# The opening's last chain in single-bank PSUM tiles, one A unit ahead of step 0 instead of two, step 0 in halves

## The chip, the cores and the metric

The kernel runs on one core of one Trainium2 chip. The metric is the device time of one execution in microseconds (us); it is given as the median of several runs. All times inside an execution are from one profiled execution, counted from its first instruction. The engines are named as in the profile: PE (TensorE's matmuls), PEld (its weight loads), DVE (VectorE), ACT (ScalarE), POOL (GpSimd) and SP (SyncE, which here only issues DMAs).

## The reference

`x` holds 8 images of 3008 rows with 256 columns. Each image is transformed along its rows, mixed by a complex 256x256 matrix, shrunk towards zero and transformed back; all rows then go through a two-layer network with an ELU between.

```python
X = np.fft.rfft(x, axis=1)                       # x: (8, 3008, 256)
Yr = Xr @ w_r - Xi @ w_i + b_r
Yi = Xr @ w_i + Xi @ w_r + b_i
Yr = np.sign(Yr) * np.maximum(np.abs(Yr) - 0.01, 0.0)   # Yi likewise
y = np.fft.irfft(Yr + 1j * Yi, n=3008, axis=1)
h = y.reshape(24064, 256) @ w_in                 # w_in: (256, 2048)
g = np.where(h > 0.0, h, np.exp(np.minimum(h, 0.0)) - 1.0)
out = g @ w_out                                  # w_out: (2048, 256)
```

## The kernel before

**Units.** The Fourier transforms are done as matmuls, 3008 being 47 x 64. Per image there are five kinds of units, each a few matmuls into a PSUM tile that ACT or DVE then copies (evicts) to SBUF:

- A (6 per image, `unit_A`, line 146): the first transform of `x`. Two units fill one tile `A` of 8 columns, which SP stores to the DRAM tensor `DA` (line 159). `A` comes from a pool with two buffers of tag `A`, so the tile after next can be written only when the store has read this one.
- X (8, `unit_X`): the second transform, from `Z`, which is `DA` read back in another layout (`load_Z`, two loads).
- M (12, `unit_M`): the complex mixing and the shrinking, giving `Y`.
- B (6, `unit_B`, line 246): the first inverse transform, into `Bz`, stored by SP to the DRAM tensor `DB`.
- Y (8, `unit_Y`, line 347): the second inverse transform, from `Bs`, which is `DB` read back (`load_Bs`, four loads `w` = 0 to 3), into `yT`.

**Opening.** Image 0 goes through all of its units before the first step. The order of the opening is written out by hand, and every engine and SP's DMA queue run their instructions in that order. B units 0, 1 and 2 of image 0 are needed soonest; `turn_B` and `turn_back` take them to `Bs` by small matmuls instead of through DRAM. Then come Y units 0 and 1, `fB(2)` (B unit 2 for the other rows, whose store completes `DB`), and the three remaining loads of `Bs`. `spare_A(0)` and `spare_A(1)` are A units 0 and 1 of image 1, done in the gaps; `spare_A(1)` also issues the store of that tile to `DA`, ahead of the loads of `Bs` in SP's queue. PSUM is held in the opening by `pre2` (two tiles of two banks), `pre1` (three of one) and `pre0` (one). `unit_ps("tps", True)` and `unit_ps("yps", True)` are tiles of two banks, whose halves ACT and DVE copy.

**Steps.** The network is then worked off in 376 steps, 47 per image. Step `i` (`front`, line 790) computes one pair of 128 hidden columns for a block of 512 rows: four matmuls into `hps`. ACT takes its exponential into `Et`; then either DVE clamps it (line 829) and forms `gT` (line 817), or, in a step without other work ("bare"), ACT, POOL and DVE do it in halves (lines 799, 827 and 815). Two steps later `back` (line 848) multiplies `gT` into the output. PSUM now has `psF` (one tile of two banks, for the units), `psH` (two of two, for `hps`) and `psO` (two of one).

**Who works beside the steps.** `plan(b)` writes out, for the 47 steps beside image `b`, which unit goes into which step: kind `a` (A units of the next image, only for `b` = 0) and the loads come in `f1`, after the step's `hps` matmuls; all others in `f0`, before them. For `b` = 0 the order is: A units 2 to 5 of image 1 in steps 0 to 3, Y units 2 to 7 of image 0, X, M and B units of image 1, A units 0 to 2 of image 2, Y units 0 and 1 of image 1 (called `n`), A units 3 to 5 of image 2; three steps are left bare. The loads of `Bs` for image 1 follow its B unit 5, the loads of `Z` follow the last A unit.

Of the kernel before, what the change touches and what calls it, by code (L numbers as in the profile page):

```python
# [10 lines left out]
BF16 = mybir.dt.bfloat16  # L11
# [8 lines left out]
N1 = 47  # L20
# [9 lines left out]
def kernel(  # L30
# [53 lines left out]
    xtp = ctx.enter_context(tc.tile_pool(name="xtp", bufs=1))  # L84

    ctx.enter_context(tc.manual_schedule())
    first = ExitStack()
    pre2 = first.enter_context(tc.tile_pool(name="pre2", bufs=2, space=bass.MemoryType.PSUM))
    pre1 = first.enter_context(tc.tile_pool(name="pre1", bufs=3, space=bass.MemoryType.PSUM))
    pre0 = first.enter_context(tc.tile_pool(name="pre0", bufs=1, space=bass.MemoryType.PSUM))  # L90
# [182 lines left out]
        nc.sync.dma_start(Bs[r0:], dv[r0:, 8 * w : 8 * w + 8, :])  # L273
        Bs_of[b, w] = Bs

    def spare_A(u):

        got = []
        if u == 0:
            A_of[1, 0] = wk2.tile([P, 8, D], BF16, name="A", tag="A")  # L280
            DA_of[1] = dram.tile([NJ, P, D], BF16, name="DA", tag="DA")
        for j in range(2):
            ps = pre1.tile([P, 512], F32, name="aps1", tag="mps1")
            c = 4 * u + 2 * j
            nc.tensor.matmul(ps[:], lhsT=M1[:], rhs=xts[0][:, c : c + 2, :], start=True, stop=True)
            got.append((A_of[1, 0][:, c : c + 2, :].rearrange("p n d -> p (n d)"), ps))

        def store(first_on_dve):
            for j, (A, ps) in enumerate(got):
                evac(A, ps[:], first_on_dve or bool(j))  # L290
            if u:
                nc.sync.dma_start(DA_of[1][0:8].rearrange("j p d -> p j d"), A_of[1, 0][:])

        return store

    NT = 3
    turned = []

    def turn_B(v):

        if not turned:
            turned.append(wk3.tile([P, 2, 8, 16 * NT], BF16, name="yb", tag="yb"))
        Y, T = Y_of[0, v], turned[0]
        ps = unit_ps("tps", True)
        to = ps[:, :, 0:P].rearrange("p s (t m q g) -> p s t q g m", t=2, m=8, q=2)
        for pp in range(2):
            for dt in range(2):
                for c in range(2):
                    for s in range(2):
                        nc.tensor.matmul(  # L310
                            to[:, s, dt, pp],
                            lhsT=Y[
                                s * N2 : s * N2 + N2, pp, c * D + dt * P : c * D + dt * P + P
                            ],
                            rhs=M3[s * N2 : s * N2 + N2, 2 * v + pp, c, :].rearrange(
                                "p (g m) -> p g m", g=4
                            )[:, :, 0:8],
                            start=(c == 0), stop=(c == 1),
                        )
        Tv = T[:, :, :, 16 * v : 16 * v + 16].rearrange("p t m (q s g) -> p s (t m) q g", q=2, s=2)  # L320
        fr = ps[:, :, 0:P].rearrange("p s (n q g) -> p s n q g", q=2, g=4)
        for s, copy in enumerate((nc.scalar.copy, nc.vector.tensor_copy)):
            copy(Tv[:, s], fr[:, s])

    def turn_back(dt):

        ps = unit_ps("tps", True)
        for j in range(8):
            nc.tensor.matmul(
                ps[0 : 16 * NT, j // 4, j % 4 * P : j % 4 * P + P],  # L330
                lhsT=turned[0][:, dt, j, :], rhs=idm[:], start=True, stop=True,
            )
        for h, copy in enumerate((nc.scalar.copy, nc.vector.tensor_copy)):
            copy(
                Bs_of[0, 0][0 : 16 * NT, 4 * h : 4 * h + 4, dt * P : dt * P + P],
                ps[0 : 16 * NT, h, :].rearrange("p (m d) -> p m d", d=P),
            )

    def unit_Y(b, u, alone=False, on_dve=False):
        w, dt = u // 2, u % 2  # L340
        if u == 0:
            yT_of[b] = late2.tile([P, 2, S], BF16, name="yT", tag="yT")
        yT, Bs = yT_of[b], Bs_of[b, w]
        ps = unit_ps("yps", alone)
        psv = ps[:].rearrange("p a (k j) -> p (a k) j", j=P)
        for j in range(8):
            nc.tensor.matmul(  # L347
                psv[:, j, 0 : 2 * N1], lhsT=Bs[:, j, dt * P : dt * P + P], rhs=M4[:],
                start=True, stop=True,
            )  # L350
        yv = yT[:, dt, w * WT : w * WT + WT].rearrange("p (r j) -> p r j", j=8)
        pv = psv[:, :, 0 : 2 * N1].rearrange("p j r -> p r j")
        if alone:
            for h in range(2):
                evac(yv[:, h * N1 : h * N1 + N1], pv[:, h * N1 : h * N1 + N1], bool(h))
        else:
            evac(yv, pv, on_dve)

    busy = constp.tile([P, 512], BF16, name="busy")
    nc.vector.memset(busy[:], 1.0)  # L360
# [307 lines left out]
    def fB(v, on_dve=False):  # L668
        unit_B(0, v, alone=True, on_dve=on_dve)
# [54 lines left out]
    first_M(2, 1, True)  # L724
    turn_B(1)
    let_go()
    fB(1, True)
    load_w_in(3)
    turn_B(2)
    spare_A(0)(False)  # L730
    M4v = M4[:].rearrange("p (a h) -> p a h", h=2)
    for h, w in enumerate((w40, w41)):
        nc.gpsimd.tensor_scalar(
# [1 line left out]
        )  # L735
    gate(Bs_of[0, 0][64:96, 0, 0:1])
    load_w_out(1)
    turn_back(0)
    turn_back(1)
    store = spare_A(1)  # L740
    unit_Y(0, 0, alone=True)
    idle_pe(1)
    unit_Y(0, 1, alone=True)
    fB(2)
    store(True)
    scale_w_in(1, True, 1)
    for w in range(1, 4):
        load_Bs(0, w)
    first.close()

    psF = ctx.enter_context(
        tc.tile_pool(name="psF", bufs=1, space=bass.MemoryType.PSUM, reuse_waits="tile")
# [122 lines left out]
    def plan(b):  # L875

        f0 = [[] for _ in range(PER)]
        f1 = [[] for _ in range(PER)]
        n1, n2 = b + 1, b + 2
        mid = [("X", u) for u in range(8)] + [  # L880
            ("M", 0, 0), ("M", 0, 1), ("M", 1, 0), ("M", 1, 1), ("B", 0), ("M", 2, 0),
            ("M", 2, 1), ("B", 1), ("M", 3, 0), ("M", 3, 1), ("B", 2), ("M", 4, 0),
            ("M", 4, 1), ("B", 3), ("M", 5, 0), ("M", 5, 1), ("B", 4),
            ("A", 0), ("B", 5), ("A", 1), ("A", 2), ("A", 3), ("A", 4),
        ]
        if n1 < B:
            lead, seq = 0, [("y", u) for u in range(2, 6)] + mid
            if b:
                seq.insert(20, ("y", 6))
                seq.insert(24, ("y", 7))  # L890
                xs = (3, 8, 13)
                seq += [("A", 5), ("n", 0), ("n", 1)]
            else:
                seq = (
                    [("a", u) for u in range(2, 6)] + [("y", u) for u in range(2, 8)]
                    + [u for u in mid if u[0] != "A"]
                    + [("A", 0), ("A", 1), ("A", 2), ("n", 0), ("n", 1)]
                    + [("A", u) for u in range(3, 6)]
                )
                xs = (9, 12, 15)  # L900
        else:
            lead, seq = 0, [("y", u) for u in range(2, 8)]
        for t, u in enumerate(seq, lead):
            if u[0] == "y":
                f0[t].append(put("Y", b, u[1]))
            elif u[0] == "n":
                f0[t].append(put("Y", n1, u[1]))
            elif u[0] == "a":
                f1[t].append(put("A", n1, u[1]))
            elif u[0] == "A":  # L910
                if n2 < B:
                    f0[t].append(put("A", n2, u[1]))
            else:
                f0[t].append(put(u[0], n1, *u[1:]))
            if u == (("A", 1) if b and n2 < B else ("B", 5)):
                f1[t] += [(load_Bs, (n1, w)) for w in range(4)]
            if u == ("A", 5) and n2 < B:
                f1[t] += [(load_Z, (n2, s0, s1)) for s0, s1 in ((0, 8), (8, NS))]
        if b == 0:
            for t in range(4):  # L920
                f1[t + 1].append((scale_w_in, (2 + t // 2, True, t % 2)))
            f1[4] += [(load_Z, (1, s0, s1)) for s0, s1 in ((0, 8), (8, NS))]
            f1[xs[0]].append((lambda: gate(Z_of[1][:, 16, 0:1]), ()))
        if n2 < B:
            for ci in range(3):
                f1[xs[ci]].append((load_x, (n2, ci)))
        return f0, f1
# [3 lines left out]
    for i in range(n + LAG):  # L931
        if i < n:
            r = i % PER
            if r == 0:
                f0, f1 = plan(i // PER)
                used = [bool(u0 or u1) for u0, u1 in zip(f0, f1)]
            free = not used[r]
            bare = bare + 1 if free else 0
            calm = free and (i >= n - 2 or (r + 2 < PER and not used[r + 1] and not used[r + 2]))
            for f, a in f0[r]:  # L940
                f(*a)
            on_act = any(f is unit_M for f, a in f0[r])
            h = front(i, calm and bare % 3 == 1, on_act, free and i > 0)
        finish_elu()
        if i < n:
            for f, a in f1[r]:
# [1 line left out]
            split = i > LAG and (i - LAG) % NPAIR == NPAIR - 1  # L948
            if split:
                back(i - LAG, True)  # L950
            elu(i, *h, free and i > 0, on_act)
        else:
            split = False
        if i >= LAG and not split:
# [31 lines left out]
```

## Time and profile before

| | us |
|---|---|
| median of 3 runs | 910.41 (909.49 to 911.92) |
| profiled execution, its own time | 909.7 |
| its span, first to last instruction | 907.9 |
| first matmul of step 0 (line 790) | 54.07 |
| eviction of A unit 4 of image 1 on ACT | 60.25 |
| first Y unit beside the steps (line 347) | 63.57 |
| Y unit 0 of image 1 (line 347) | 148.12 |

A line of the timeline has the start, the duration, the engine, the source line, the operation, what it writes and reads, the shapes and the count of instructions merged; in brackets the time for which the engine stood idle before it, and what released it. "SPq" is SP issuing DMAs. A line of the windows has, for each engine, busy time and count, then the granted PE clock (1.00 is full), the DMA engines' share and GB/s. A piece of the chain of waits has start, duration and what the time went to. When a DMA has landed is in the trace's landing records, which no view prints for each DMA; where such a time is used, the text says so.

### The profile page before, as it was taken

The numbers are of one execution on the slowest core, as the hardware profiler recorded it, in microseconds if no ns is written. First come the engines' busy times: TensorE is split into PE (matmuls) and PEld (weight loads), VectorE is DVE, ScalarE is ACT, GpSimd is POOL, SyncE is SP. The second block draws the span as 40 slices with busy tenths as digits, with TensorE's granted clock in tenths as the row PEclk, the third lists the DMA queues.
The fourth block names the chain that finished last, engine by engine and source line by source line (L and its number), as shares of the span: only waits on it lengthen the run. The fifth ranks groups of instructions, "written<-read, shape, count | busy, mean of one in ns | idle before, by whom it ended". The sixth has DMA issues, their size and how long they took to land.

```text
span 907.9 us, 17273 instructions
## 1 busy us (share of the span) xinstructions
PE 885.0 (97%) x6665; PEld 653.1 (72%) x6768; DVE 721.0 (79%) x901; ACT 698.9 (77%) x855; POOL 313.0 (34%) x436
## 2 busy tenths in 40 slices
PE   9879999999999999999999999999999999999997
PEld 3457667876678676876678766787667866777775
DVE  8779778887788778887788877888778877778776
ACT  6678778787878788788787888878787877777664
POOL 7700440233331431405404153133332134443664
PEclk9999999999999999999999999999999999999999
DMA  8997025721383215722176031752228111221011
GB/s 270 310 258 233 24 70 174 222 70 48 93 232 117 70 48 155 199 88 93 53 204 186 25 106 58 205 167 80 61 73 229 32 40 47 84 80 48 24 47 47
DMA packets 90623, 106.06 MB, mean 117 GB/s; under 512 B 5270, under 2 KB 81308, under 8 KB 87180
## 3 DMA queue, kind: packets, MB, share of 16 engines
q1 hardware_dynamic: 84284, 77.42, 30.5%
q0 software_dynamic: 5968, 27.26, 9.1%
q8 instruction: 53, 0.87, 0.4%
q10 hardware_dynamic: 288, 0.26, 0.1%
q14 instruction: 30, 0.25, 0.1%
HBM read 55.12 MB, written 49.81 MB: 116 GB/s over the span
## 4 chain that ended last, share of the span: by engine, by line
PE 84%; DVE 5%; ACT 4%; DMA 3%; issue 2%; POOL 0%; SPq 0%; DVEq 0%; ACTq 0%; POOLq 0%
PE ps_o L848 34%; PE hps L790 33%; PE mps L194 9%; PE yps L347 2%; PE bps L246 2%; PE aps L146 2%; PE xps L177 2%; DVE gT L817 1%; ACT Bz L259 1%; ACT Et L804 1%; DMA Bs<-DB 1%; DVE Et L829 1%; DMA Z<-DA 1%; ACT Et L801 1%; DMA DB<-Bz 1%
## 5 line engine op out<-in xcount | busy, mean ns | idle before, releaser
L848 PE MATMUL ps_o<-w_out_r,gT 128*128 128x256 f32 x3008 | 476.9, 301 | 0.2 <-DVE gT L815 0.2
L848 PEld LDWEIGHTS ps_o<-w_out_r,gT 128*128 128x128 f32 x3008 | 403.6, 189 | 49.9 <-DVE osb L859 1.3
L790 PE MATMUL hps<-yT,w_in_s 128*128 128x512 bf16 (+7 forms) x1651 | 382.3, 351 | 6.6 <-ACT Bz L259 1.1
L815 DVE SCALAR_TENSOR_TENSOR gT<-Et,hps 128x512 fp32r<-128x512 f32 (+1 forms) x268 | 220.3, 850 | 74.1 <-POOL Et L827 37.6
L817 DVE SCALAR_TENSOR_TENSOR gT<-hps,Et 128x1024 fp32r<-128x1024 f32 x200 | 244.6, 1223 | 16.2 <-DVE Et L829 0.5
L790 PEld LDWEIGHTS <-w_in_s 128*128 128x128 bf16 x1728 | 141.6, 98 | 129.7 <-issue 22.7
L804 ACT ACTIVATE Et<-hps 128x1024 f32<-128x1024 f32 x200 | 206.1, 1030 | 11.1 <-PE hps L790 4.4
L827 POOL TENSOR_SCALAR Et<-Et 128x512 f32<-128x512 f32 x183 | 109.2, 615 | 219.4 <-ACT Et L799 219.4
L829 DVE TENSOR_SCALAR Et<-Et 128x1024 f32<-128x1024 f32 x200 | 138.6, 693 | 48.0 <-ACT Et L804 39.9
L212 POOL TENSOR_SCALAR clip<-yb 128x512 f32<-128x512 f32 x84 | 51.8, 616 | 318.1 <-DVE yb L204 286.0
L799 ACT ACTIVATE Et<-hps 128x512 f32<-128x512 f32 x184 | 99.9, 595 | 62.8 <-PE hps L790 62.1
L801 ACT ACTIVATE Et<-hps 128x1024 f32<-128x1024 f32 x84 | 86.2, 1027 | 71.8 <-PE hps L790 70.2
L213 POOL TENSOR_TENSOR Y<-yb,clip 128x512 bf16<-128x512 f32 x84 | 107.3, 1277 | 7.0
L802 ACT ACTIVATE Et<-Et 128x1024 f32<-128x1024 f32 x84 | 88.9, 1058 | 2.7
L204 DVE TENSOR_TENSOR yb<-mps,bias_bc 128x512 f32<-128x512 f32 x89 | 61.3, 689 | 35.5 <-PE mps L194 23.2
L129 ACT CAST XT<-xps 128x768 bf16<-128x768 f32 x61 | 48.8, 799 | 15.4 <-PE xps L177 15.4
L129 ACT CAST yT<-yps 128x752 bf16<-128x752 f32 (+1 forms) x64 | 49.8, 779 | 13.4 <-PE yps L347 13.2
L129 ACT CAST A<-aps 128x1024 bf16<-128x1024 f32 (+1 forms) x47 | 47.2, 1004 | 13.2 <-PE aps L146 11.6
L194 PE MATMUL mps<-wcat_r,XT 128*128 128x512 bf16 x180 | 55.6, 384 | 0.8 <-ACT Bz L259 0.3
L194 PE MATMUL mps<-wcat_s,XT 128*128 128x512 bf16 x182 | 54.9, 379 | 0.7
L194 PEld LDWEIGHTS <-XT 128*128 128x128 bf16 x384 | 30.8, 98 | 29.6 <-DVE XT L127 0.6
L259 ACT CAST Bz<-bps 128x1024 bf16<-128x1024 f32 x46 | 46.1, 1001 | 2.8 <-PE bps L246 2.8
(121 smaller groups left out, 414.3 us busy)
## 6 DMA issues: line engine op xcount, KB each, us to landing
xt<-in_x_dram POOLq DMA_DIRECT2D x21, 1024.0 KB, 7.5
out_dram<-osb SPq DMA_DIRECT2D x158, 128.0 KB
Bs<-DB SPq DMA_DIRECT2D x31, 384.0 KB
DA<-A SPq DMA_DIRECT2D x21, 512.0 KB
DB<-Bz SPq DMA_DIRECT2D x21, 512.0 KB
Z<-DA SPq DMA_DIRECT2D x7, 1152.0 KB
Z<-DA SPq DMA_DIRECT2D x11, 384.0 KB
xt<-in_x_dram POOLq DMA_DIRECT2D x6, 512.0 KB, 5.8
```

Source lines behind the costliest of these rows:

```text
L129: nc.scalar.copy(dst, src)
L194: nc.tensor.matmul(ps, lhsT=XT[:, dt, c, o : o + P], rhs=wm[:, dt, :], start=(not biased and m == 0 and dt == 0), stop=(m == 1 and dt == 1),)
L213: nc.gpsimd.tensor_tensor(Y_of[b, q][:, i, :], yb, clip[:], ALU.subtract)
L790: nc.tensor.matmul(hps[:, s, c0:c1], lhsT=w_in_s[:, dt, ft * P : ft * P + P], rhs=yT_of[b][:, dt, t0 : t0 + c1 - c0], start=(dt == 0), sto ...
L799: nc.scalar.activation(E_[:, s], hps[:, s], AF.Exp)
L801: nc.scalar.activation(E_, hps[:], AF.Relu, scale=-1.0)
L804: nc.scalar.activation(E_, hps[:], AF.Exp)
L815: nc.vector.scalar_tensor_tensor(o, e, -1.0, h, ALU.add, ALU.max)
L817: nc.vector.scalar_tensor_tensor(o, h, 0.0, e, ALU.max, ALU.add)
L827: eng.tensor_scalar(E_[:, s], E_[:, s], 1.0, 0.0, ALU.min, ALU.max)
L829: nc.vector.tensor_scalar(E_, E_, 1.0, -1.0, ALU.min, ALU.add)
L848: nc.tensor.matmul(po[q][:, i_ % 2, :], lhsT=gT[:, s, i_ * P : i_ * P + P], rhs=w_out_r[:, ft, :], start=(ft == 0 and i_ % 2 == 0), stop=( ...
```

## The change

- `spare_A` loses its argument: only A unit 0 of image 1 is done ahead, into two single-bank tiles (`lateA`), copied by ACT and DVE. It issues no store. A unit 1 goes to the front of `plan(0)`: units 1 to 5 of kind `a` take steps 0 to 4, and the store of the first tile `A` is issued by unit 1, in step 0. All that follows in `plan(0)` up to B unit 5 comes one step later; of the A units of image 2, two instead of three stand ahead of `n`, and four behind it. The loads of `x` and `Z` move one step too. Two steps are left bare.
- From `turn_B(2)` on, the opening uses PSUM pools of single banks: `lateA` (2), `chain` (4) and `lateB` (2). ACT copies one bank and DVE another. These banks are later `psF`, `psH` and `psO`, in this order.
- `turn_B(0)` and `turn_B(1)` are copied by ACT alone, `fB(1)` too.
- `fB(2)` becomes `last_B(2)`, which comes after the first Y units on PE, in two single banks copied by DVE.
- `first_Y` replaces `unit_Y(0, 0)` and `unit_Y(0, 1)`; its halves are four of the eight columns each. `idle_pe(1)` between them is gone.
- Step 0 is done in halves, as a bare step is.

```diff
-    def spare_A(u):
+    def two_banks(pool, n):
+        return [pool.tile([P, 512], F32, name=n, tag=n) for _ in range(2)]
+
+    def spare_A():
...
-            if u:
-                nc.sync.dma_start(DA_of[1][0:8].rearrange("j p d -> p j d"), A_of[1, 0][:])
+    def last_B(v):
+
+        Bz, Y = Bz_of[0, v // 2], Y_of.pop((0, v))
+        ps = two_banks(lateB, "lateB")
...
+        def store():
+            for s in range(2):
+                evac(Bv[:, s], ps[s][:].rearrange("p (q d) -> p q d", d=D), True)
+            nc.sync.dma_start(
+                DB_of[0][4 * v : 4 * v + 4].rearrange("k p d -> p k d"), Bz[:, o : o + 4, :]
+            )
...
-        for s, copy in enumerate((nc.scalar.copy, nc.vector.tensor_copy)):
-            copy(Tv[:, s], fr[:, s])
+        for s in range(2):
+            evac(Tv[:, s], ps[s].rearrange("p (n q g) -> p n q g", q=2, g=4), split and bool(s))
...
+    def first_Y(dt):
...
+        for h in range(2):
+            ps = one_bank()
+            pv = ps[:].rearrange("p (k j) -> p k j", j=P)[:, :, 0 : 2 * N1]
+            for j in range(4):
+                nc.tensor.matmul(
+                    pv[:, j], lhsT=Bs_of[0, 0][:, 4 * h + j, dt * P : dt * P + P], rhs=M4[:],
+                    start=True, stop=True,
+                )
+            evac(yv[:, :, 4 * h : 4 * h + 4], pv.rearrange("p j r -> p r j"), bool(h))
...
-    fB(1, True)
+    fB(1)
     load_w_in(3)
-    turn_B(2)
-    spare_A(0)(False)
...
     load_w_out(1)
+    first.close()
+    lateA, chain, lateB = (
+        second.enter_context(
+            tc.tile_pool(name=n_, bufs=k_, space=bass.MemoryType.PSUM, reuse_waits="tile")
+        )
+        for n_, k_ in (("lateA", 2), ("chain", 4), ("lateB", 2))
+    )
+    turn_B(2, True)
     turn_back(0)
     turn_back(1)
-    store = spare_A(1)
-    unit_Y(0, 0, alone=True)
-    idle_pe(1)
-    unit_Y(0, 1, alone=True)
-    fB(2)
-    store(True)
+    keep_A = spare_A()
+    first_Y(0)
+    first_Y(1)
+    keep_B = last_B(2)
+    keep_A()
+    keep_B()
     scale_w_in(1, True, 1)
     for w in range(1, 4):
         load_Bs(0, w)
-    first.close()
+    second.close()
...
-                    [("a", u) for u in range(2, 6)] + [("y", u) for u in range(2, 8)]
+                    [("a", u) for u in range(1, 6)] + [("y", u) for u in range(2, 8)]
                     + [u for u in mid if u[0] != "A"]
-                    + [("A", 0), ("A", 1), ("A", 2), ("n", 0), ("n", 1)]
-                    + [("A", u) for u in range(3, 6)]
+                    + [("A", 0), ("A", 1), ("n", 0), ("n", 1)]
+                    + [("A", u) for u in range(2, 6)]
                 )
-                xs = (9, 12, 15)
+                xs = (10, 13, 16)
...
-            f1[4] += [(load_Z, (1, s0, s1)) for s0, s1 in ((0, 8), (8, NS))]
+            f1[5] += [(load_Z, (1, s0, s1)) for s0, s1 in ((0, 8), (8, NS))]
...
-            h = front(i, calm and bare % 3 == 1, on_act, free and i > 0)
+            h = front(i, calm and bare % 3 == 1, on_act, free or i == 0)
...
-            elu(i, *h, free and i > 0, on_act)
+            elu(i, *h, free or i == 0, on_act)
```

## The prediction

> **What bounds the kernel now.** I read the page first, then the chain of waits, then the timeline of the opening, of SP's queue and of the PE.
>
> ```profile
> PE 885.0 (97%) x6665; PEld 653.1 (72%) x6768; DVE 721.0 (79%) x901; ACT 698.9 (77%) x855; POOL 313.0 (34%) x436
> ```
>
> PE is busy for 885 of 907.9 us: time is won only where PE waits, and a wait put into PE's queue is paid in full. PE waits in the opening (48 to 64 us), which the change rewrites:
>
> ```profile
> 49.28 1.06 ACT L334 CAST Bs<-tps 48x512 bf16<-48x512 f32 x2 [0.30 <-PE tps L329]
> 49.89 1.28 DVE L334 CAST Bs<-tps 48x512 bf16<-48x512 f32 x2 [0.57 <-ACT Bs L334]
> 51.75 1.10 DVE L127 CAST yT<-yps 128x376 bf16<-128x376 f32 x2 [0.58 <-ACT yT L129]
> 53.01 1.01 ACT L259 CAST Bz<-bps 128x1024 bf16<-128x1024 f32 x1 [0.73 <-PE bps L246]
> 54.07 1.02 PE L790 MATMUL hps<-yT,w_in_s 128*128 128x512 bf16 x4 [1.10 <-ACT Bz L259]
> 60.25 1.00 ACT L129 CAST A<-aps 128x1024 bf16<-128x1024 f32 x1
> 62.51 1.00 ACT L129 CAST A<-aps 128x1024 bf16<-128x1024 f32 x1
> 63.57 0.49 PE L347 MATMUL yps<-M,Bs 96*128 96x94 bf16 x8 [0.59 <-ACT A L129]
> ```
>
> DVE's half of an eviction begins when ACT's half ends (0.57, 0.58), and step 0's matmuls (54.07) wait for the eviction of `fB(2)`, whose banks they take. 63.57 is the first Y unit of the steps, y2; I call its time the landmark. Now SP's queue:
>
> ```profile
> 54.04 0.36 SPq L262 DMA_DIRECT2D DB<-Bz  x1
> 54.46 0.50 SPq L292 DMA_DIRECT2D DA<-A  x1
> 58.15 1.26 SPq L273 DMA_DIRECT2D Bs<-DB  x3
> 59.51 4.41 SPq L159 DMA_DIRECT2D DA<-A  x2
> ```
>
> SP issues nothing from 54.96 to 58.15: the loads of `Bs` wait there for the store of `DB`. The first store of `DA` (columns 0 to 7 of image 1) stands before that wait. The trace's landing records give 58.08 for `DB`, 59.47 for this `DA`, 62.01, 64.82 and 65.88 for the three `Bs`, and 67.18 for the next `DA`.
>
> **The change, part by part.**
>
> *The chain to step 0.* Until `turn_back` little moves: ACT takes both halves of `turn_B(0)` and `(1)` and all of `fB(1)`, which I cost at nothing, as PE runs units of its own meanwhile; `turn_back` then starts near 48.2 (before: 48.61). If ACT's extra halves (3 of 0.27) show, it is 0.4 later. From there DVE is the slower lane. PE: `turn_back` 1.07 to 49.27, two matmuls of A 0.47 to 49.74. DVE: its first `Bs` half ends by about 50.15, the first `yT` half can start at 49.74+0.53 (a matmul group's start to its eviction, 50.72 to 51.25) = 50.27, two halves of 0.55: 51.37. Step 0's matmuls start at 51.4 instead of 54.07; not later than 51.9 if the strided `yT` writes cost more. The 8 matmuls of `last_B` (0.61) run under these evictions, and its own evictions now leave other banks than step 0's.
>
> *Five A units instead of four.* Before, step 0 to the landmark takes 63.57-54.07 = 9.50 with four. One more such step is 2.26 (58.27 to 60.53), and step 0 in halves takes back about 0.1 of it (ACT 1.09, POOL 1.19, DVE 1.28 overlap, gT is 0.5 earlier, but ACT's evictions follow one another anyway): 11.7. The landmark would be at 51.4+11.7 = 63.1: 0.5 gained.
>
> *The A unit after the first stage.* It falls among bare steps: a step with A takes 2.30 (155.51 to 157.81), a bare one 1.83 (157.81 to 159.64): 0.47 more.
>
> *n0.* Unit B5 moves one step towards n0, the first Y of image 1, since only two A units stand between.
>
> ```profile
> 139.31 1.03 ACT Bz L259
> 140.36 3.24 DMA DB<-Bz
> 143.73 4.35 DMA Bs<-DB
> 148.12 0.51 PE yps L347 x8
> ```
>
> From B5's eviction to n0 it takes 7.8 whatever PE does. PE's wait there grows from 0.3 to about 2.6, by the A step that is taken away. It adds nothing to the sum: n0 keeps its distance from B5, and B5 from the landmark.
>
> *The store of DA, the term that decides.* In the changed kernel this store is no longer issued by `spare_A`, but by unit 1 in step 0, after the three `load_Bs` in SP's queue. It is passed by all three and stands behind their wait for `DB`. Who waits for it: unit 4's eviction writes the buffer of tag `A` (two buffers) from which this store reads; before, it ran at 60.25, 0.8 after the store had landed. In the built order of the changed kernel ACT's copy of unit 4 waits on that store's semaphore; behind it on ACT stand step 4's Exp and unit 5's eviction, and PE waits for both.
>
> The sum: `yT` done on DVE 51.37, then 0.64 and twice 0.64 for lateA and lateB: `DB` issued at 53.3, landed 4.04 later as before: 57.35. `Bs` x3 and then `DA` issued 1.43 later (58.08 to 59.51): 58.8. Behind three `Bs` loads a `DA` took 7.67 (59.51 to 67.18); behind four, 7.8 (145.73 to 153.53). I take off 0.66, half of the 1.3 in which the old first `DA` still ran beside those loads: landed at 65.8. The bounds: alone a `DA` took 4.33 (159.34 to 163.67), landing 63.1; with `DB` no earlier than now and 7.8, 67.3.
>
> Without this, unit 4's eviction would start at 51.4+8.4 (62.51-54.07) = 59.8. So ACT is held for 6.0. After the landing: eviction, Exp, eviction of unit 5 at intervals of 0.92, then y2: 2.9 later, at 68.7. Against 63.57 this is 5.1, with the 0.47 it is 5.6.
>
> What else moves with it is covered: step 0's two clamps go to POOL, which is idle from 50 to 66; the loads of `Z` follow the last `DA` (issued at 68.7, then 5.1 as at 63.5, then 4.1 and 8.6 for the two parts, as landed at 72.99 and 77.53 after 68.88), so 78 and 82.4, while X0 comes 12.9 after the landmark as before, at 81.6, and the unit that needs the second part 4.5 later. If that cover were gone, each us would count in full.
>
> *The clock.* PE stands still from about 60.9 (end of step 4's hps) to 66.9, six us.
>
> ```profile
> 1.45 4.02 PE L366 MATMUL ips<-busy 128*128 128x512 bf16 x9 [1.45 <-DVE busy L360]
> 8.17 0.82 PE L366 MATMUL ips<-busy 128*128 128x512 bf16 x3
> 904.00:905.00 1.00, 0.00 (x0) 0.00 (x0) 0.00 (x0) 0.00 (x0) 0.00 (x0) 0.96 0.40 99
> 905.00:906.00 1.00, 0.00 (x0) 0.00 (x0) 0.00 (x0) 0.00 (x0) 0.00 (x0) 0.50 1.03 325
> ```
>
> Nine matmuls at the start take 4.02, later the same matmul takes a little over 0.2; the fast rate comes at about 7.2, after 5.8 of work. At the end PE's last matmul ends at 902.6, and the granted clock (the column behind the engines) is 0.96 at 904 to 905 and 0.50 after. The gap of 1.55 at 24 us left it at 1.00. So I expect half speed after six us of rest. With 5.8 at half speed, unit 5, the back step, y2, hps and a part of the next back step take double: 2.5 lost. If it lasts 3.4, 1.3 is lost; nothing at the least, 2.95 at the most.
>
> The Trainium skill (TensorE: Matmul & The Clock Gate, Part 1) puts both at about 3.4 us, idle to slow down and busy to come back. By its figure for coming back the loss would be 1.3 rather than 2.5.
>
> *Sum.* 0.5 earlier at step 0 is inside the landmark; 5.1+0.47+2.5 = 8.1. The profiled execution took 909.7 (span 907.9): 917.8. It lies 0.7 below the median of 910.41, so 918.5 for a median.
>
> **The rivals.** All in medians.
>
> A. As summed: 918.5. Chance 0.62.
>
> B. The same wait, but the clock holds: 910.4+5.6 = 916.0. For it: no gap inside the steps of before shows a slowdown; against it: none there is over two us, and the end of the span shows one. 0.18.
>
> C. The store isn't held by the loads before it and takes what it takes alone, 4.33: y2 at 63.1+2.9 = 66.0, 2.5+0.47 more: 913.4. Against it stand both rows of a `DA` behind `Bs` loads. 0.05. [...]
>
> D. Not slower: `DA` lands before 59.8, so unit 4 never waits. Then the landmark is at 63.1, and -0.5+0.47 is nothing: 910.4. The point that decides is this landing. It would need `DB` landed by about 51 or the store ahead of the loads; against it stands SP's queue, silent for 3.2 us in the fence above. 0.12, of which 0.03 for a gain over 0.3% because the chain to step 0 or the B units come out earlier than I see.
>
> E. `DB` lands no earlier than now, and the slow clock lasts longest: 67.3 and 2.95, some 920.5 and over. 0.03.
>
> **The numbers.** 0.3% of 910.4, 2.7 us, is about what a measurement can tell from no change: the same is 907.7 to 913.1. A, B, E and most of C are slower: 0.87; D without its fast part and the rest of C the same: 0.10; faster 0.03. The range goes from C, 913.2, to E, 920.5, and leaves out D and what is above: less than 2 in 10.
>
> **What would show it.** In the changed kernel: step 0's hps near 51.4; SP's second line after `DB` is `Bs` x3, with `DA` near 58.8; a wait of ACT's copy into `A` for the DMA of `DA`, about 6, and PE idle from 61 to 67; then matmuls of hps at 0.43 each and a granted clock under 1 for some us; y2 at 68.7 or later; PE's wait at n0 2 to 3 us; one bare step less in image 0. A copy of unit 4 before 60.5 would refute A, B, C and E at once; a wait with a clock of 1.00 throughout makes it B.

## The result and the profile after

The changed kernel takes 920.05 us (median of 6 runs, 918.23 to 921.62), the kernel before 910.5 (909.49 to 911.95) in the runs beside it: the ratio is 1.0102, interval 1.0085 to 1.0118. The profiled execution took 920.67 (span 918.9), 11.0 more than that of before.

First the page's busy time, for the changed kernel:

```profile
PE 893.4 (97%) x6767; PEld 655.0 (71%) x6767; DVE 719.8 (78%) x898; ACT 699.0 (76%) x857; POOL 313.0 (34%) x436
```

PE's sum is 8.4 us larger, but records of 102 more of its instructions are in it, so it doesn't measure the loss; DVE, ACT and POOL do what they did. The loss is found in the timeline.

The timeline of the changed kernel's opening, lines that answer to those shown of before:

```profile
48.12 0.41 PE L343 MATMUL one<-M,Y 64*128 64x32 bf16 x16 [1.21 <-ACT A L259]
...
49.67 1.28 DVE L127 CAST Bs<-one 48x512 bf16<-48x512 f32 x2 [0.79 <-PE one L362]
...
51.13 1.01 DVE L127 CAST yT<-one 128x376 bf16<-128x376 f32 x2 [0.18 <-PE one L380]
...
51.90 1.10 PE L839 MATMUL hps<-yT,w_in_s 128*128 128x512 bf16 x4
...
66.92 1.01 ACT L129 CAST A<-aps 128x1024 bf16<-128x1024 f32 x1 [6.35 <-DMA DA<-A]
...
67.98 1.22 PE L146 MATMUL aps<-xt,M 128*128 128x512 f32 x2 [6.19 <-ACT A L129]
...
69.00 1.91 PE L897 MATMUL ps_o<-w_out_r,gT 128*128 128x256 f32 x8
...
70.71 0.74 PE L394 MATMUL yps<-M,Bs 96*128 96x94 bf16 x8
```

The change does what it says: DVE no longer waits for ACT's half, and step 0 starts 2.2 earlier (51.90; 54.07 before). But by y2, the landmark, the 2.2 won have become 7.1 lost (70.71; 63.57). Between them stands one wait: ACT's copy of A unit 4 into `A`, held for 6.35 by a DMA, and PE behind it for 6.19. Its cause is in SP's queue:

```profile
53.95 0.36 SPq L317 DMA_DIRECT2D DB<-Bz  x1
58.64 1.26 SPq L273 DMA_DIRECT2D Bs<-DB  x3
59.95 10.69 SPq L159 DMA_DIRECT2D DA<-A  x3
```

The first `DA` store is issued at 59.95, behind the loads of `Bs`, which stood for 4.3 in the queue until `DB` had landed (58.56 in the landing records). The loads landed at 62.58, 64.22 and 65.46, the store at 66.82, 0.10 before ACT went on.

The windows of the changed kernel (busy time and count of PE, PEld, DVE, ACT and POOL, then the granted clock, the DMA engines' share and GB/s):

```profile
62.00:64.00 2.00, 0.00 (x0) 0.00 (x0) 1.00 (x2) 0.00 (x0) 0.00 (x0) 1.00 1.01 240
64.00:66.00 2.00, 0.00 (x0) 0.00 (x0) 0.00 (x0) 0.00 (x0) 0.00 (x0) 0.59 1.06 295
...
68.00:70.00 2.00, 2.00 (x7) 1.81 (x8) 1.01 (x2) 1.62 (x2) 0.00 (x0) 0.50 0.00 0
70.00:72.00 2.00, 2.00 (x18) 1.55 (x16) 0.91 (x1) 0.77 (x2) 0.00 (x0) 0.70 0.36 116
72.00:74.00 2.00, 2.00 (x21) 1.67 (x20) 0.59 (x1) 1.66 (x3) 0.00 (x0) 1.00 0.46 146
```

PE rests from 61.8. By the trace's clock records, whose mean the windows print, the clock is at half rate from 64.36 to 71.19: it halves some 2.5 after PE's last matmul and is back 3.2 after PE resumed (67.98). In between unit 5's two matmuls take 1.22 instead of 0.73. The second place is Y unit 0 of image 1 (n0), in the timeline and the windows:

```profile
155.81 0.51 PE L394 MATMUL yps<-M,Bs 96*128 96x94 bf16 x8 [2.73 <-DMA Bs<-DB]
156.16 1.55 PE L839 MATMUL hps<-yT,w_in_s 128*128 128x512 bf16 x4
...
157.15 2.27 PE L897 MATMUL ps_o<-w_out_r,gT 128*128 128x256 f32 x8
156.00:158.00 2.00, 2.00 (x15) 1.33 (x13) 0.00 (x0) 1.04 (x2) 0.00 (x0) 0.63 1.03 262
158.00:160.00 2.00, 2.00 (x16) 1.91 (x16) 1.09 (x2) 0.77 (x1) 0.00 (x0) 0.52 1.04 281
```

The wait of 2.73 is followed by hps at 1.55 and a back step at 2.27 (1.03 and 1.27 at full clock). The milestones, all from the timelines:

| | before | after | lost so far |
|---|---|---|---|
| step 0's hps | 54.07 | 51.90 | -2.2 |
| y2 | 63.57 | 70.71 | 7.1 |
| eviction of B unit 5 (ACT) | 139.31 | 146.71 | 7.4 |
| n0 | 148.12 | 155.81 | 7.7 |
| Y unit 2 of image 1 | 165.09 | 175.47 | 10.4 |
| end of the span | 907.9 | 918.9 | 11.0 |

### The profile page after: what moved, and what is told of

Read it like the earlier page. It is cut to its first block, busy times and chain, and to the rows that moved or that the text cites. A ratio compares the mean times of both kernels' runs of the same rounds, so it can differ in the third digit from the quotient of the medians.

```text
span 918.9 us, 17373 instructions
## 1 busy us (share of the span) xinstructions
PE 893.4 (97%) x6767; PEld 655.0 (71%) x6767; DVE 719.8 (78%) x898; ACT 699.0 (76%) x857; POOL 313.0 (34%) x436
## 4 chain that ended last, share of the span: by engine, by line
PE 83%; DVE 5%; ACT 4%; DMA 4%; issue 2%; POOL 1%; SPq 0%; DVEq 0%; ACTq 0%; POOLq 0%
PE ps_o L897 33%; PE hps L839 33%; PE mps L194 9%; PE yps L394 2%; PE aps L146 2%; PE bps L246 2%; PE xps L177 2%; DVE gT L866 1%; DMA DB<-Bz 1%; DMA Bs<-DB 1%; DVE Et L878 1%; ACT Et L853 1%; ACT Bz L259 1%; ACT Et L850 1%; DMA xt<-in_x_dram 1%
## 5 line engine op out<-in xcount | busy, mean ns | idle before, releaser
L839 PE MATMUL hps<-yT,w_in_s 128*128 128x512 bf16 (+4 forms) x1728 | 389.7, 353 | 1.3 <-DVE gT L866 0.3
L129 ACT CAST A<-aps 128x1024 bf16<-128x1024 f32 x47 | 47.7, 1014 | 19.9 <-PE aps L146 11.6
L129 ACT CAST yT<-yps 128x752 bf16<-128x752 f32 x62 | 48.9, 788 | 16.8 <-PE yps L394 16.7
L194 PE MATMUL mps<-wcat_r,XT 128*128 128x512 bf16 x192 | 58.2, 384 | 1.0 <-ACT Bz L259 0.5
L194 PE MATMUL mps<-wcat_s,XT 128*128 128x512 bf16 x192 | 57.1, 379 | 0.0
```

Source lines behind the costliest of these rows:

```text
L129: nc.scalar.copy(dst, src)
L194: nc.tensor.matmul(ps, lhsT=XT[:, dt, c, o : o + P], rhs=wm[:, dt, :], start=(not biased and m == 0 and dt == 0), stop=(m == 1 and dt == 1),)
L839: nc.tensor.matmul(hps[:, s, c0:c1], lhsT=w_in_s[:, dt, ft * P : ft * P + P], rhs=yT_of[b][:, dt, t0 : t0 + c1 - c0], start=(dt == 0), sto ...
```

## The experiments

**The store ahead of the loads** (changed kernel):

```diff
-    for w in range(1, 4):
-        load_Bs(0, w)
...
+            f1[0] += [(load_Bs, (0, w)) for w in range(1, 4)]
```

> The changed kernel, with the three loads of Bs issued in step 0 behind A unit 1 instead of at the end of the opening, so that the store of the first A tile stands ahead of them in SP's queue; nothing else differs. Theory S (unit 4's eviction waits for that store, which stands behind the loads): the store is issued near 55 and lands by 61, ACT has no wait for DA, PE and its clock go through 61 to 72 without a break, y2 comes at 51.9+11.7 = 63.6 instead of 70.7, and the time falls by 7.1 to 913. The wait at n0 and the slow clock after it stay. Rival P (the opening's new tail and step 0 in halves set the pace of the A steps): y2 stays near 70 and the time near 920.

Measured: 913.95, ratio 1.0037 (1.0025 to 1.0048). SP's queue, and ACT's line of unit 4:

```profile
54.91 0.36 SPq L317 DMA_DIRECT2D DB<-Bz  x1
56.00 0.36 SPq L159 DMA_DIRECT2D DA<-A  x1
60.07 1.26 SPq L273 DMA_DIRECT2D Bs<-DB  x3
61.50 1.01 ACT L129 CAST A<-aps 128x1024 bf16<-128x1024 f32 x1
```

The same instructions in another order of one queue: no wait for the store is left, the clock is 1.00 from 60 to 74, and 6.1 of the 9.6 lost are back. In this profile y2 comes at 64.76, not at the 63.6 expected, mostly because step 0 starts only at 52.86; the wait at n0 (2.37) and the half rate behind it stay, as expected.

**The same queue, another buffer** (changed kernel; units 4 and 5 write a buffer of tag `Bz`, so that the late store holds nobody):

```diff
+            elif b == 1 and ci == 2:
+                A_of[b, ci] = wk2.tile([P, 8, D], BF16, name="Bz", tag="Bz")
```

> The changed kernel, with A units 4 and 5 of image 1 writing a tile of tag Bz instead of tag A, so that unit 4 has a buffer that no late store reads; SP's queue is untouched. Theory S: the store still lands near 67, but nobody waits for it before the load of Z; y2 at 63.6, time 913, as with the store moved. If it were the transfers themselves (traffic of the loads and the store) that hold the steps, or rival P, y2 stays near 70 and the time near 920.

Measured: 913.07, ratio 1.0028 (1.0018 to 1.0037).

```profile
58.97 1.26 SPq L275 DMA_DIRECT2D Bs<-DB  x3
60.28 1.16 SPq L161 DMA_DIRECT2D DA<-A  x2
61.85 1.00 ACT L129 CAST Bz<-aps 128x1024 bf16<-128x1024 f32 x1
```

The store is as late as in the changed kernel and lands at 67.26, and nobody waits for it. (y2 comes at 65.15 here: the clock falls in the opening, and step 0 starts at 53.31.) It is not the traffic but the buffer that the store still holds.

**The late store alone** (kernel before; `spare_A(1)` no longer issues it):

```diff
-            if u:
-                nc.sync.dma_start(DA_of[1][0:8].rearrange("j p d -> p j d"), A_of[1, 0][:])
...
     for w in range(1, 4):
         load_Bs(0, w)
+    nc.sync.dma_start(DA_of[1][0:8].rearrange("j p d -> p j d"), A_of[1, 0][:])
```

> The kernel before, with only one thing done: the store of the first A tile is issued behind the three loads of Bs. Theory S: it is issued near 59.5 and lands near 67, unit 4's eviction goes from 60.25 to 67, PE's clock falls, y2 goes from 63.57 to about 70.9, the time from 910.5 to about 917.8. Rival P: nothing of the new opening is in this kernel, so 910.5.

Measured: 918.59, ratio 1.0088 (1.0073 to 1.0103).

```profile
60.54 0.43 SPq L747 DMA_DIRECT2D DA<-A  x1
...
68.33 1.01 ACT L129 CAST A<-aps 128x1024 bf16<-128x1024 f32 x1 [6.19 <-DMA DA<-A]
```

One DMA, moved behind three others in its queue, costs the kernel before 8.1 by the medians, clock included (0.55 from 66 to 68, 0.50 to 72). The times of this one profile are no measure of it: step 0 starts at 55.35 instead of 54.07, and the clock is at half rate from 55.97 to 59.38 already, so y2 comes at 72.12 and not at the 70.9 expected. In the changed kernel the same order was worth 6.1, by the first run. I take the price of this term to lie between them; then the rest of the change costs some 1.5 to 3.4.

**n0 one A unit sooner, alone** (kernel before):

```diff
-                    + [("A", 0), ("A", 1), ("A", 2), ("n", 0), ("n", 1)]
-                    + [("A", u) for u in range(3, 6)]
+                    + [("A", 0), ("A", 1), ("n", 0), ("n", 1)]
+                    + [("A", u) for u in range(2, 6)]
```

> The kernel before, with the two Y units n0 and n1 of image 1 moved one A unit nearer to B unit 5 (two A units between instead of three), as the change has it. As the prediction had it, the wait at n0 grows from 0.3 to 2.6 with nothing gained for it here: 912.8 if the clock holds. If a wait of 2.6 is enough for the clock to fall, as the trace of the changed kernel seems to show behind n0, another 1.7: 914.5. If neither matters, 910.5.

Measured: 914.1 (911.38 to 915.7, 10 runs), ratio 1.004 (1.0029 to 1.0051). In the profiled execution (911.83, mean clock 0.999) n0 comes at 148.35 after a wait of 2.32 and the clock stays at 1.00. One other execution has a mean clock of 1.0 and took 911.38; the eight others, at 0.995 to 0.997, took 913.56 to 915.7. So the order by itself costs 2.1 between the two profiled executions (an A step goes behind n0, and no bare step is taken away in exchange), and in most executions some 2 to 4 more go with a lower clock. That this loss lies behind n0 is not shown for the eight executions, of which there is only the mean clock; it lies there in the profiles of the changed kernel and of the store ahead of the loads.

**PE kept busy in the store's wait** (changed kernel; 20 idle matmuls, whose result nobody uses):

```diff
+            f1[4].insert(0, (fill_pe, (5, 20)))
```

`fill_pe`, whose code is not shown, puts 20 matmuls of 128x512 into the tile that step 5 then overwrites.

> The changed kernel, with 20 idle matmuls of 128x512 (0.22 each, 4.3 together) into step 5's hps tile, which that step overwrites, ahead of A unit 5 in step 4: PE works through most of the wait for the store, while the wait itself stays. Theory S with the clock as a cost of its own: the eviction of unit 4 still starts near 67, the granted clock stays at 1.00 from 64 to 72, y2 comes 2.9 after the store's landing instead of 3.8. The prediction's term makes this 2.5 in all: 917.5. As I read the trace of the changed kernel (0.9 until y2, 0.25 behind it), it is 1.15: 918.9. If the clock costs nothing there, because ACT sets the pace until y2: 920.0.

Measured: 920.02, ratio 1.0112 (1.0098 to 1.0125).

```profile
64.07 4.48 PE L830 MATMUL hps<-busy 128*128 128x512 bf16 x20 [1.07 <-DVE gT L878]
...
68.20 0.82 PE L146 MATMUL aps<-xt,M 128*128 128x512 f32 x2
...
70.12 0.49 PE L394 MATMUL yps<-M,Bs 96*128 96x94 bf16 x8 [0.17 <-ACT A L129]
```

The clock stays at 1.00 from 60 to 74, but the matmuls run until 68.55. Unit 4's copy ended at 67.33, so they hold up unit 5 by 0.9, which is what the clock would have taken. The run says that PE's rest is what lowers the clock there, and nothing on the price.

**PE kept busy ahead of n0** (the store ahead of the loads, and 10 idle matmuls):

```diff
+            f0[39].insert(0, (fill_pe, (39, 10)))
```

> store_first, with 10 idle matmuls (2.2) into step 39's hps tile ahead of n0, which is where PE waits 2.4 for the loads of Bs. Nothing is taken away from the wait, so n0 comes where it came. If the slow clock behind n0 is a cost, as in store_first (half speed from 150 to 154), the time falls by up to 1.7 from 913.95, to 912.3; in executions whose clock held anyway nothing is won. If that slow clock is hidden: 913.95.

Measured: 914.44, ratio 1.0046 (1.0029 to 1.0063), against 1.0037 without them: no gain. Behind n0 the clock was 1.00 now, but this profile shows other falls: one in the opening (0.73 from 48 to 50 and 0.50 from 50 to 52) and one from 799.85 to 803.26, behind a wait of 1.97 for the loads of `Bs`. The medians therefore tell nothing on the price behind n0. The profiles do: from n0 to Y unit 2 of image 1 it takes 18.07 here and 19.42 without the idle matmuls.

**n0 back behind three A units** (the store ahead of the loads; Y unit 6 shares a step with unit 5, which frees one), first with step 0 in halves, then whole; lines of the edit:

```diff
-                    [("a", u) for u in range(1, 6)] + [("y", u) for u in range(2, 8)]
+                    [("a", u) for u in range(1, 6)] + [("y", u) for u in (2, 3, 4, 5, 7)]
-                    + [("A", 0), ("A", 1), ("n", 0), ("n", 1)]
-                    + [("A", u) for u in range(2, 6)]
+                    + [("A", 0), ("A", 1), ("A", 2), ("n", 0), ("n", 1)]
+                    + [("A", u) for u in range(3, 6)]
...
+            f1[8].append(put("Y", 0, 6))
```

> store_first, and in the plan Y unit 6 of image 0 shares step 8 with Y unit 5 (one before, one behind the step's hps), so that all behind it, B unit 5 too, comes one step sooner, three A units stand between B unit 5 and n0 again, and three steps are left bare. Both waits that the runs so far show are gone: unit 4 does not wait, n0 waits 0.3 to 0.5, the clock is 1.00 throughout. Against store_first it wins the filled wait (2.2) and the clock (up to 1.7) and a bare step's shorter time: 909.5 to 910. Against the kernel before it has y2 at the same time with one step more behind it, and pays a doubled step: between 908.6 and 910.5, so 909.5. If the opening and the steps behind n0 had a further cost that I do not see, over 911.

Measured: 909.88, ratio 0.9993 (0.9984 to 1.0002). n0 comes at 148.43, after a wait of 0.32 of its first weight load (0.30 before). Of the loss against the kernel before nothing is left.

> doubled, with step 0 done whole on ACT and DVE as in the kernel before, so that the halves stand by themselves. By the prediction's working the halves bring gT of step 0 forward by 0.5, of which 0.1 reaches y2: 0.1 slower than doubled, not to be told from it. If the POOL step in the chain costs more than it saves: faster by up to 0.5.

Measured: 909.5, ratio 0.9987 (0.9976 to 0.9998): step 0 in halves gives nothing that shows.

**The opening's rest filled** (the last kernel, with four idle matmuls):

```diff
     fB(1)
+    idle_pe(4)
```

> The base is the doubled kernel with step 0 done whole (909.5 in its own runs), and four idle matmuls (4 x 0.22 = 0.9) are put on PE behind B unit 1, into the rest of 1.2 in which PE waits for ACT's eviction of that unit. Nothing else differs. In four of the seven profiles with the changed opening that stand so far the granted clock was 0.50 from about 49 to 52.5 and step 0's hps came 1.2 to 1.4 later than in the three others. Theory: this rest of PE, which the changed kernel has and the kernel before has not (its PE is busy for 1.23 of the two us from 46 to 48, the changed one for 0.61), lets the clock fall in some of the executions; filled, the clock stays at 1.00 from 48 to 54 in every one, hps of step 0 starts at 51.9 to 52.3, and with about half of the executions relieved of 1.2 the median is 0.3 to 0.9 lower, 908.6 to 909.2. Rival: what differs between the executions is the arrival of loads; then the start of step 0 goes on varying, and the median stays at 909.5 (or is higher, if the idle matmuls delay turn_B(2)).

Measured: 908.27 (907.85 to 909.91), ratio 0.998 (0.9971 to 0.9989), faster than both kernels. PE's timeline up to `turn_back` (the second of the `one` rows), first of the kernel with step 0 in halves, in whose profile the clock fell there, then of this one:

```profile
48.15 0.41 PE L343 MATMUL one<-M,Y 64*128 64x32 bf16 x16 [1.21 <-ACT A L259]
49.05 1.87 PE L362 MATMUL one<-idm,yb 128*48 128x128 bf16 x16 [0.49 <-DVE yb L127]
```

```profile
46.74 1.04 PE L409 MATMUL ips<-busy 128*128 128x512 bf16 x4
48.02 0.41 PE L343 MATMUL one<-M,Y 64*128 64x32 bf16 x16 [0.25 <-ACT A L259]
48.92 1.05 PE L362 MATMUL one<-idm,yb 128*48 128x128 bf16 x16 [0.49 <-DVE yb L127]
```

`turn_back` takes 1.05 instead of 1.87, and step 0 starts at 51.79 instead of 53.35. The clock is 1.00 from 46 to 54. In the one profile of the kernel that it copies, with step 0 whole, the clock held too: `turn_back` takes 1.05 there, and step 0 starts at 52.01. The two ratios, 0.998 and 0.9987, have overlapping intervals, so a gain by the idle matmuls (0.0007 of 910, some 0.6) is likely, not shown; the gain over the kernel before is.

> The changed kernel with the same four idle matmuls behind B unit 1. Theory: the opening's clock stays at 1.00, the store of A's first tile still lands after the three loads of Bs, unit 4's eviction still waits some 6, and both later falls of the clock stay: 919.0 to 919.8 against 920.05. Rival: 920.05 or more.

The same four in the changed kernel: 919.91, ratio 1.0099 (1.0084 to 1.0113), not to be told from 1.0102. The store's wait is there in full (7.04 on ACT). Of the two later falls, both expected to stay, the profile has only the first, and it is longer: the half rate lasts from 66.80 to 73.62, until 5.0 after PE resumed, while behind n0 (a wait of 2.39) the clock holds.

> The changed kernel with idle matmuls in all three rests of PE: 4 behind B unit 1, 14 (3.1) ahead of A unit 5 where unit 4's eviction waits for the store, 10 (2.3) ahead of Y unit 0 of image 1. It measures what the clock costs in all; the waits themselves stay. Theory: the clock stays at 1.00 throughout; the spell behind the store's wait (1.15), that behind Y unit 0 (1.75) and a share of the one in the opening (0.3 to 0.9) are taken away, 3.2 to 3.8 of 9.6, which gives 916.2 to 916.9, and y2 comes 2.9 to 3.0 after the landing of the store instead of 3.8. Rival, that the clock is a by-mark and only the waits cost: 919.5 to 920.5. If the idle matmuls overrun their rest, the time lies between.

All three rests filled in the changed kernel: 917.64, ratio 1.0081 (1.0069 to 1.0094). Behind n0 and in the opening the clock holds. The 14 matmuls ahead of unit 5 end at 65.78 and unit 5 comes only at 67.63, and the clock falls there all the same (0.58 from 68 to 70; from y2 to the next Y unit it takes 3.09). So it is some 2 less than the changed kernel (0.0021 of 910; the intervals overlap a little), not the 3.2 to 3.8 expected, and of the loss 7.6 stays, that fall included.

## Why the prediction came out as it did

Direction, mechanism and size held: 918.5 was forecast for the median and 920.05 measured, the profiled execution at 920.67 instead of 917.8. That the size came so near is in part luck, as the sum at the end shows. Step by step:

- **The store of `DA` decides: right.** SP's order, the wait of ACT's copy (6.0 forecast, 6.35 measured), PE's rest behind it and the landing behind three loads (7.0 after issue forecast, 6.9 measured) are as written. Three runs show it from three sides: the order undone gives 6.1 back, another buffer 7.0, and the order alone makes 8.1. Rival B is refuted by the half rate behind the wait, C by the 6.9, D by ACT's wait. The first half of E came true: `DB` landed at 58.56, no earlier than the 58.08 of before. But the store landed before E's 67.3, and the clock took less there than its 2.95.
- **Step 0 at 51.4: nearly.** It came at 51.90, the later bound given. The step that failed is "cost at nothing" for ACT's extra halves: `turn_B(2)` waits 1.21 for ACT's eviction of `fB(1)`, and `turn_back` starts at 49.02, not 48.2. So `DB` was issued at 53.95 (53.3) and flew 4.6 (4.04), and the store landed at 66.82 (65.8).
- **y2 at 68.7: 70.71.** 1.0 of it is that landing and 0.1 the time from it to the copy; the rest is the 3.8 from the copy's start to y2 instead of 2.9. That 0.9 is the clock (unit 5's matmuls at 1.22 and the back step at 1.91 hold up what follows them), which the prediction has as a term of its own.
- **The clock, 2.5: mis-sized.** Behind the store's wait it cost 0.9 up to y2 and 0.2 behind it (y2 to the next Y unit 2.38; 2.15 later), 1.1 together. The half rate did not last the 5.8 read from the start of the execution but 3.2, counted from PE's return; in two other profiles with this wait (the late store alone, and the changed kernel with four idle matmuls) it was 3.6 and 5.0. The 3.4 of the Trainium skill (TensorE: Matmul & The Clock Gate, Part 1) was the better figure here.
- **n0 "adds nothing to the sum": wrong.** The distance from B5's eviction to n0 held (8.1 from its end; 7.8 before), and the wait came as forecast (2.73; 2.6). But a rest of that length may also halve the clock. The prediction's own rows had it: PE's last matmul ends at 902.84 (not 902.6), and at 904.93, 2.1 later, the clock was at half rate, so a wait of 2.6 had no claim to cost nothing. From n0 to Y unit 2 of image 1 it took 19.66; in the profiles of the changed kernel with four idle matmuls and with all three rests filled, where the clock held, 18.04 both times. So 1.6 of the 2.7 lost there is clock.
- **The A unit after the first stage, 0.47: too small.** 18.04 against 16.97 before is 1.07 without any clock. One bare step in the changed kernel's stretch takes 2.26, where those of before take 1.83, and the last step with an A unit takes 2.46, where the others take 2.30. Why these two are longer I have not pinned down.

The sum for the profiled execution: 7.1 up to y2, of which 0.9 is clock (5.1 forecast, without it), 0.6 up to n0, of which 0.2 is clock (none), 2.7 from there to Y unit 2 (0.47), 0.6 up to the end, unexplained (none). The clock at both places together is 2.7, close to the 2.5 forecast for one: two errors that hid each other.

## What to carry to other kernels

When a step is moved, follow every DMA that it issues into its new place in the queue, and ask two things: what does a DMA ahead of it wait for, and which engine needs the buffer that it holds. A store whose buffer is soon needed goes ahead of a load that waits, or gets a buffer of its own; the earlier start that the change wins on PE is worth nothing if this is late. A rest of PE of some 2 us, or two short ones close together, should be priced twice, as itself and as the slow matmuls that may follow it; where the rest can't be removed, idle matmuls that end with it, neither after it nor long before, may pay.

## What the runs showed of the hardware

How short a rest can halve PE's clock was not expected, nor that the same rest does so only in some executions. In the opening PE rests 1.21 and 0.49 with 0.41 of work between: the granted clock fell to 0.50 some 2 us after the first rest's start in four of seven profiles, and in none of the three with four idle matmuls there. Ahead of n0 a wait of 2.3 to 2.7 was followed by a fall in the changed kernel, in the one with the store ahead of the loads (0.66 from 150 to 152) and in the one filled in the store's wait, and not with the third buffer, with n0 sooner alone, or with the four idle matmuls in the opening. After the long rest the fall came 2.5 us after PE's last matmul in one profile and 5.0 in another.

The clock records say what sorts these cases. In all 13 profiles each spell at one rate, the last of a record apart, lasts a whole multiple of 3.413 us: in the changed kernel two such stretches at half rate (64.36 to 71.19), then 25 at full, one at half (156.52 to 159.94) and 222 at full. So the rate changes only at the ends of these stretches, and where they lie differs from execution to execution (the first of them starts anywhere from 4.4 to 10.7 us). What sorts the falls is PE's work inside one stretch. Of some 3400 stretches at full rate every one with less than 1.5 us of it was followed by half rate, and none with more than 1.9; between the two both occur (PE's busy time is the profile's, which models the ends). The changed kernel had 0.84 from 60.95 to 64.36 and 0.70 from 153.11 to 156.52; ahead of n0 it was 1.4 with the store ahead of the loads, where the clock fell, and 1.55 with the third buffer, where it held. The same rest can fall inside one stretch or be shared by two.

The clock comes back in the same way, at the end of a stretch with enough work (3.1 or more in all that were followed by the full rate, 1.59 at most in those that were not). That is why it took 3.2, 3.6 and 5.0 after PE's return. The Trainium skill (TensorE: Matmul & The Clock Gate, Part 1) has the activity judged in windows of 3.4 us that run freely, whatever the kernel does, and the 3.413 and the differing places agree with it.
